# Sigmoid attention with a bilinear feed-forward network: every engine's work in a written order, decoding of the weights dealt out in single operations, no GpSimd work, the first group of products over 28 bursts

## The chip, the cores and the metric

One core of a Trainium2 chip runs the whole program. The metric is the time of one execution on the device in microseconds (us), the median of several runs. "Span" is the time from the first to the last instruction in the one profiled execution.

## What is computed

Attention over 8 batches, 12 heads, 448 positions and 64 values a head, with a sigmoid in the softmax's place; then a network of four weight matrices without a nonlinearity but the product of two branches.

```python
scores = q @ k.transpose(0, 1, 3, 2) / np.sqrt(64) - np.log(448)
attn   = 1.0 / (1.0 + np.exp(-scores))
x      = (attn @ v).transpose(0, 2, 1, 3).reshape(8 * 448, 768)
out    = ((x @ w1) * (x @ w2)) @ w3 @ w_out       # w1, w2: 768x1024, w3: 1024x1024, w_out: 1024x768
```

The four weights arrive as 64-bit numbers, which the kernel reads as pairs of 32-bit words and decodes itself.

## The kernel before

**Attention.** The work is cut into 168 items: for each batch and each quad of four heads seven items of one 128-row chunk for two heads, one of them (`None`) the short last chunk of all four heads. A burst is two items; 84 bursts run, numbered from 0. In each burst TensorE (PE) makes the scores of its items (`scores` L161, `short_scores` L171), ScalarE (ACT) makes two sigmoids (`sigmoid` L151), and PE multiplies the sigmoids of the burst before with v (`attend` L184, `attend_short` L192). A matrix goes to PE as a rounded high part and the rest as a low part (`split`, L66 and L67); `split_pair` does it for q and k on VectorE (DVE).

**The operands of the first products.** When a pair of heads is done, `combine` copies it out of PSUM on ACT (L215) and makes with DVE the sums and differences of blocks (L218) that seven products in Strassen's manner want (`PRODUCTS`: A11, S2, A12, S3, S1, A22, S4). Each is split into high and low (`split_operand`); for `kc == 1` the low part is made by GpSimd (POOL). For the groups after the first, all but the last wait in the list `due`, and six a burst are taken from it in bursts without products.

**The first products.** Two batches are a group, four groups in all. `up` makes for each of 8 column chunks seven products of nine matmuls (L342), so 504 a group. After each product DVE or ACT reads the sum out of PSUM (L324, L327, L350, L356); two PSUM banks, or four with the last group, take turns, so the reading of a product has to be over when the second product after it starts. Results go to memory (`g_dram`, L328). Groups begin at bursts 23, 44 and 65 and run over 16 bursts with 32 matmuls a burst; the fourth follows the last burst.

**The weights.** `prepare_weights` loads raw words of w1 and w2 (L71), ACT takes the magnitude (`magnitude`, L76), DVE decodes in six operations (`decode`, L83 to L99), DVE makes four differences (L268), and seven split operands (ACT's cast, POOL's low part) are stored to `w_dram` (L285 loads them again for each group through a ring of 7 buffers). One step of this stream is a whole decoding or a whole split. `load_job` and `decode_job` do the like for w3 and w_out in 32 jobs from burst 37 on: a load in one burst, and in the next the magnitude, the decoding and the store (L302).

**Order.** PE and the transfer queue of SyncE (SP) run in the order in which the code is written (`manual_schedule(engines={ET.PE, ET.SP})`); DVE, ACT and POOL are ordered by the scheduler. On SP an instruction that waits holds up all transfers written behind it.

**After the groups.** The weights of w3 and w_out are multiplied with each other (L602), and seven products in Strassen's manner give the output (L727).

## Time and profile before

| | |
|---|---|
| runs | 1127.82, 1128.65 and 1133.06 us, median 1128.65 |
| profiled execution, its own time | 1130.64 us |
| its span | 1128.5 us |
| its mean granted TensorE clock | 0.961 of full speed |
| bytes moved | 226.40 MB, mean 201 GB/s |

The profile has for each engine the time in which it was busy, and for each wait what ended it. Matmuls overlap, so PE's busy time is not a measure of how near it is to its peak: a stretch is judged by how far apart equal pieces of its work start. A wait costs only where PE comes to stand still behind it.

### The profile page before, as it was taken

How to read it: one execution, taken by the hardware profiler on the slowest of the kernel's cores; microseconds unless marked ns; L12 is line 12 of the kernel's file. 1: busy time of each engine (PE TensorE's matmuls, PEld its weight loads, DVE VectorE, ACT ScalarE, POOL GpSimd, SP SyncE). 2: the span in 40 equal slices, each digit the busy share in tenths (PEclk: the TensorE clock that was granted, in tenths of full speed). 3: DMA queues.
4: the chain of work that ended last, by engine and by line, in shares of the span. 5: the costliest groups of instructions: out<-in, count | busy, mean ns of one | idle time of the engine just before them, and what ended most of it. 6: DMA issues, size and time to landing. Idle time of an engine off the chain costs nothing.

```text
span 1128.5 us, 14274 instructions
## 1 busy us (share of the span) xinstructions
PE 1016.1 (90%) x5250; PEld 769.3 (68%) x5250; DVE 677.6 (60%) x1038; ACT 367.1 (33%) x518; POOL 125.1 (11%) x88
## 2 busy tenths in 40 slices
PE   7786897679977899898879999989999999999998
PEld 4232565557744666665456676669999999999997
DVE  6898676753586544457854545774444665656663
ACT  4575333333242232323423223321112342323230
POOL 0446223340120000001200000110000000000000
PEclk9899998989998899999889999989999999999999
DMA  6964987978734877766377777638874203344312
GB/s 201 305 218 153 316 275 252 323 265 297 223 106 126 289 255 238 240 190 210 98 258 250 240 245 245 197 121 294 293 255 156 103 9 115 131 139 149 121 49 74
DMA packets 122437, 226.40 MB, mean 201 GB/s; under 512 B 10752, under 2 KB 80384, under 8 KB 122368
## 3 DMA queue, kind: packets, MB, share of 16 engines
q1 hardware_dynamic: 122368, 225.49, 60.0%
q8 instruction: 42, 0.69, 0.3%
q14 instruction: 27, 0.22, 0.1%
HBM read 170.39 MB, written 55.05 MB: 200 GB/s over the span
## 4 chain that ended last, share of the span: by engine, by line
PE 59%; DVE 18%; DMA 14%; issue 4%; ACT 2%; SPq 2%; POOL 0%; ACTq 0%; DVEq 0%; POOLq 0%
PE up L342 26%; PE up L727 18%; PE up L602 6%; DMA raw<-w3T 4%; PE av L184 4%; PE sp L161 4%; DMA raw<-w_out 3%; DMA raw<-w 3%; DMA w<-w_dram 2%; DVE raw L96 2%; DVE f L91 2%; DVE raw L83 2%; DVE f L99 2%; ACT f L76 1%; DVE f L88 1%
## 5 line engine op out<-in xcount | busy, mean ns | idle before, releaser
L342 PE MATMUL up<-hS,w 128*128 128x448 f32 x768 | 248.1, 382 | 52.0 <-DVE u L324 18.2
L151 ACT ACTIVATE a<-sp,bias 128x896 f32<-128x896 f32 x168 | 162.4, 1005 | 228.2 <-PE sp L161 204.7
L342 PE MATMUL up<-hA,w 128*128 128x448 f32 x576 | 188.2, 380 | 21.9 <-ACT p L350 10.4
L342 PEld LDWEIGHTS up<-hS,w 128*128 128x128 f32 x768 | 148.3, 194 | 87.0 <-DVE u L324 22.4
L727 PE MATMUL up<-gh,wo 128*128 128x448 f32 x672 | 192.2, 367 | 0.0
L342 PE MATMUL up<-lS,w 128*128 128x448 f32 x384 | 145.2, 378 | 1.2 <-POOL lS L67 0.8
L342 PEld LDWEIGHTS up<-hA,w 128*128 128x128 f32 x576 | 110.9, 193 | 46.8 <-ACT p L350 11.9
L727 PEld LDWEIGHTS up<-gh,wo 128*128 128x128 f32 x672 | 126.1, 188 | 11.3
L184 PE MATMUL av<-a,vv 128*64 128x448 f32 x576 | 132.2, 574 | 0.0
L727 PE MATMUL up<-gl,wo 128*128 128x448 f32 x336 | 123.2, 367 | 0.0
L342 PE MATMUL up<-lA,w 128*128 128x448 f32 x288 | 108.8, 378 | 0.0
L324 DVE TENSOR_TENSOR u<-up,p 128x448 f32<-128x448 f32 x64 | 39.8, 622 | 104.1 <-PE up L342 103.3
L83 DVE TENSOR_SCALAR raw<-raw 128x768 uint32<-128x768 uint32 (+2 forms) x48 | 25.8, 538 | 100.1 <-ACT f L76 100.0
L161 PE MATMUL sp<-high 64*128 64x448 f32 x288 | 65.5, 450 | 20.0 <-ACT a L151 16.9
L342 PEld LDWEIGHTS up<-lS,w 128*128 128x128 f32 x384 | 74.7, 195 | 12.1 <-issue 4.2
L184 PEld LDWEIGHTS av<-a,vv 128*64 128x64 f32 x576 | 35.0, 141 | 68.5 <-issue 68.5
L161 PEld LDWEIGHTS sp<-high 64*128 64x128 f32 x288 | 28.5, 194 | 68.9 <-ACT a L151 40.2
L76 ACT ACTIVATE f<-raw 128x768 f32<-128x768 f32 (+2 forms) x48 | 34.0, 708 | 122.4 <-DMA raw<-w_out 31.2
L67 POOL TENSOR_TENSOR lA<-A,hA 128x448 fp32r<-128x448 f32 x12 | 21.2, 1764 | 457.3 <-DVE hA L66 457.3
L727 PEld LDWEIGHTS up<-gl,wo 128*128 128x128 f32 x336 | 63.1, 188 | 5.6
L342 PEld LDWEIGHTS up<-lA,w 128*128 128x128 f32 x288 | 55.8, 194 | 10.9 <-issue 6.3
L67 DVE TENSOR_TENSOR gl<-gf,gh 128x896 fp32r<-128x896 f32 x40 | 41.9, 1087 | 31.3 <-ACT gh L66 31.3
(78 smaller groups left out, 1348.2 us busy)
## 6 DMA issues: line engine op xcount, KB each, us to landing
w<-w_dram SPq DMA_DIRECT2D x224, 384.0 KB, 4.7
w_dram<-wo SPq DMA_DIRECT2D x56, 384.0 KB, 4.4
g_dram<-c SPq DMA_DIRECT2D x64, 224.0 KB, 2.6
gf<-g_dram SPq DMA_DIRECT2D x16, 896.0 KB, 5.4
raw<-w SPq DMA_DIRECT2D x16, 768.0 KB, 8.6
qk<-qT SPq DMA_DIRECT2D x48, 224.0 KB, 4.5
qk<-kT SPq DMA_DIRECT2D x48, 224.0 KB, 4.7
out<-o_sb SPq DMA_DIRECT2D x48, 224.0 KB, 2.0
```

The lines of the kernel that those rows point to most:

```text
L67: lo_engine.tensor_tensor(out=dst_lo, in0=src, in1=dst_hi, op=ALU.subtract)
L76: nc.scalar.activation(f, raw[..., 1].bitcast(F32), AF.Abs, scale=HW_SCALE)
L83: nc.vector.tensor_scalar(out=high, in0=high, scalar1=0x80000000, scalar2=0x80000000, op0=ALU.bitwise_and, op1=ALU.bitwise_xor,)
L91: nc.vector.scalar_tensor_tensor(out=fb, in0=fb, scalar=3, in1=high, op0=ALU.logical_shift_left, op1=ALU.bitwise_xor)
L96: nc.vector.scalar_tensor_tensor(out=r, in0=low, scalar=2.0 ** -52, in1=r, op0=ALU.mult, op1=ALU.mult)
L151: nc.scalar.activation(dst, src, AF.Sigmoid, bias=bias[:n], scale=scale)
L161: nc.tensor.matmul(sp[:, j], k[rows, 1, at:at + P], q[rows, 0], start=m == 0, stop=m == 2)
L184: nc.tensor.matmul(acc[cols, :S], vv[:, c, at:at + D], a[:, j], start=u == 0 and c == 0, stop=u == 1 and c == NC - 2,)
L324: nc.vector.tensor_tensor(out=out, in0=a, in1=b, op=ALU.add)
L342: nc.tensor.matmul(a, w[:, i, kc], x, start=bool(start) and kc == 0 and m == 0, stop=bool(stop) and kc == KH - 1 and m == 2, skip_group_ch ...
L602: nc.tensor.matmul(acc, a[:, jc], w[:, jc, ms], start=(jc == 0 and m == 0), stop=(jc == NF - 1 and m == 2),)
L727: nc.tensor.matmul(acc, w[:, fc, ms], g[:, fc], start=start and fc == 0 and m == 0, stop=fc == NH - 1 and m == 2, skip_group_check=True,)
```

## The change

All five engines keep the written order until the last group is out. POOL gets no work; its low parts go to DVE. `decode` gives up control after each of its six operations, and so do the differences and splits of the weights (`finish_weights`). Outside the products two such single operations are taken a burst; beside the first group `beside` takes 3 or 4 behind each product's sum, and beside the second and third group two operations of w3's and w_out's decoding (`prepare_rest`) or one operand of the list `groups`. The casts of the first group's operands and every second one of the others' move to ACT, and so does q's and k's high part in bursts with products. The groups run over bursts 25 to 52, 58 to 66 and 71 to 79, with 18, 56 and 56 matmuls a burst. The weights' ring has 6 buffers instead of 7, `c11` and `c22` one instead of two, and the stores of results are issued one product later.

```diff
-        split(high, low, qk, nc.vector.tensor_copy, nc.vector)
+        split(high, low, qk, hi_engine, nc.vector)
...
     def split_operand(g, name, kc, src):
-        split(h, l, src, nc.vector.tensor_copy, nc.gpsimd if kc == 1 else nc.vector)
+        turn = g > 0 and len(ops[g]) % 2
+        split(h, l, src, nc.vector.tensor_copy if turn else nc.scalar.copy, nc.vector)
...
+    def late(g, kc):
+        a11, a12, s1, a22 = (xf.pop((g, name, kc)) for name in ("A11", "A12", "A21", "A22"))
+        split_operand(g, "S1", kc, s1)
+        yield
+        total(a11, s1, a11, ALU.subtract)
+        split_operand(g, "S2", kc, a11)
+        yield
+        if g > 0:
+            split_operand(g, "A12", kc, a12)
+            yield
+        total(a12, a12, a11, ALU.subtract)
+        split_operand(g, "S4", kc, a12)
+        yield
+        split_operand(g, "A22", kc, a22)
+        yield
...
     def prepare_weights():
...
+                for step, _ in enumerate(decode(raw[i], f)):
+                    if step == 4 and (i, fc) != (1, NF - 1):
+                        nxt = magnitude(raw[1 - i], p1, 3)
+                    if step == 5 and fc + 1 < NF:
+                        raw[i] = load(fc + 1, i)
+                    yield
+                    for _ in range(2 if (i, step) != (0, 0) else 1):
+                        if next(extras, None):
+                            yield
+            take(extras, 100)
+            extras = finish_weights(fc, fs)
...
-                split(wo[:, 0], wo[:, 1], src, nc.scalar.copy, nc.gpsimd)
+            split(wo[:, 0], wo[:, 1], src, nc.scalar.copy, nc.vector)
...
-    RING = 7
+    RING = 6
...
+        for i, (_, dst) in enumerate(jobs):
+            for step, _ in enumerate(decode(raw[i % 2], f)):
+                if step == 0 and store:
+                    nc.sync.dma_start(out=store[0], in_=store[1])
+                if step == 2 and i + 1 < len(jobs):
+                    following = magnitude(raw[(i + 1) % 2], p2[0], 3)
+                yield
+            store = dst, f
+            raw[i % 2] = load(i + 2)
+            f = following
...
-    order.enter_context(tc.manual_schedule(engines={ET.PE, ET.SP}))
+    ALL = {ET.PE, ET.SP, ET.Activation, ET.DVE, ET.Pool}
+    order.enter_context(tc.manual_schedule(engines=ALL))
...
+    spans = ((25, 53), (58, 67), (71, 80))
+    CHANGE = 53
...
+    def beside(g, n):
+        if not take(change, 1):
+            if g == 0:
+                take(weights, 3 + n % 5 % 2)
+            else:
+                take(rest, 2)
...
+        for g, (at, end) in enumerate(spans):
+            if k == at:
+                filler = up(g)
+            if at <= k < end:
+                n = GROUP * (k + 1 - at) // (end - at) - GROUP * (k - at) // (end - at)
+                take(filler, n + (10 if k == end - 1 else 0))
+                if k == end - 1:
+                    change = groups(g + 1)
+                break
+        else:
+            take(change, 4)
+            take(weights, 2)
```

What moves is best seen in the instructions of an engine as they stand in its queue. DVE in the second group of products, before (`u` and `c` are the sums of the products, `raw` and `f` the decoding):

```order
L324 TENSOR_TENSOR u_3455<-up,p 128x448
L83 TENSOR_SCALAR raw<-raw 128x512
L88 TENSOR_SCALAR f<-f 128x512
L91 SCALAR_TENSOR_TENSOR f<-f,raw 128x512
L95 TENSOR_SCALAR raw<-f 128x512
L96 SCALAR_TENSOR_TENSOR raw<-raw 128x512
L99 TENSOR_TENSOR f<-f,raw 128x512
L83 TENSOR_SCALAR raw<-raw 128x384
L324 TENSOR_TENSOR u_3529<-up,p 128x448
```

and now:

```order
L398 TENSOR_TENSOR u_3605<-up,p 128x448
L93 SCALAR_TENSOR_TENSOR f<-f,raw 128x512
L98 TENSOR_SCALAR raw<-f 128x512
L100 SCALAR_TENSOR_TENSOR raw<-raw 128x512
L104 TENSOR_TENSOR f<-f,raw 128x512
L398 TENSOR_TENSOR u_3637<-up,p 128x448
L83 TENSOR_SCALAR raw<-raw 128x512
L89 TENSOR_SCALAR f<-f 128x512
L67 TENSOR_TENSOR low<-qk,high 128x896
L398 TENSOR_TENSOR c_3680<-up,u_3637 128x448
L93 SCALAR_TENSOR_TENSOR f<-f,raw 128x512
L98 TENSOR_SCALAR raw<-f 128x512
```

Before, seven operations of decoding stand between two sums; now two behind each product, so four where ACT reads the sum between (`low` is a part of q and k).

SP's queue in the second group, before (L285 loads the operands of products, L71 raw words, L302 stores decoded ones, L126 is q and k):

```order
L302 DMA w_dram<-f 128x512
L71 DMA raw<-w3T 128x4x256
L126 DMA qk<-qT 128x448
L126 DMA qk<-kT 128x448
L126 DMA qk<-qT 128x448
L126 DMA qk<-kT 128x448
L285 DMA w<-w_dram 128x768 x4
L302 DMA w_dram<-f 128x512
L285 DMA w<-w_dram 128x768 x2
```

and now (L344, L71 and L367 in the same parts; L411 stores results):

```order
L71 DMA raw<-w3T 128x4x256
L367 DMA wo_dram<-f 128x384
L344 DMA w<-w_dram 128x768 x2
L139 DMA vv<-vL 128x3x256
L145 DMA vs<-vL 64x128 x2
L344 DMA w<-w_dram 128x768
L71 DMA raw<-w3T 128x4x256
L367 DMA wo_dram<-f 128x384
L344 DMA w<-w_dram 128x768 x3
L411 DMA g_dram<-c_4137 128x448
```

The store of a decoded job stood ahead of the next raw load and, here, of four loads of operands, and waited for the last operation of its own decoding; it now comes one job later, behind the raw load, which waits for that operation instead of it.

ACT at the end of the second batch, in the first stage, before (`A` is an operand's copy, `a` a sigmoid, `wo` the high part of a weight):

```order
L151 ACTIVATE a<-sp,bias 128x896 x2
L215 COPY A_855<-av 128x448
L151 ACTIVATE a<-sp,bias 128x896 x2
L66 CAST wo<-t_794 128x384
L66 CAST wo<-f 128x384
L151 ACTIVATE a<-sp,bias 128x896 x2
L215 COPY A_940<-av 128x448
L66 CAST wo<-t_796 128x384
```

and now (`hS` and `hA` are the high parts of operands):

```order
L156 ACTIVATE a<-sp,bias 128x896 x4
L246 COPY A_876<-av 128x448
L66 CAST hS_879<-A_648 128x448
L66 CAST hS_884<-A_283 128x448
L66 CAST hS_889<-A_463 128x448
L66 CAST hA_893<-A_876 128x448
L156 ACTIVATE a<-sp,bias 128x896 x2
L246 COPY A_927<-av 128x448
```

The four casts of a finished pair of heads stand now between the copy and the sigmoids of the next burst; before they were DVE's.

## Rows read from the trace of the kernel before

**Rows 1.** The busy time by engine, from the page: us, share of the span, number of instructions.
```profile
PE 1016.1 (90%) x5250; PEld 769.3 (68%) x5250; DVE 677.6 (60%) x1038; ACT 367.1 (33%) x518; POOL 125.1 (11%) x88
```

**Rows 2.** Busy time in the eight stages of the program: start and end in us, length, busy us and number of instructions of PE, PEld, DVE, ACT and POOL, then the granted clock as a share of full speed, the share of the DMA engines and GB/s.
```profile
6.30:115.50 109.20, 85.18 (x497) 34.75 (x496) 94.32 (x125) 65.00 (x88) 48.49 (x28) 0.91 0.68 223
115.50:315.90 200.40, 169.93 (x856) 122.74 (x854) 122.40 (x175) 66.61 (x100) 47.82 (x39) 0.93 0.80 272
315.90:336.50 20.60, 16.59 (x111) 6.90 (x110) 16.84 (x32) 10.99 (x15) 5.54 (x4) 1.00 0.44 134
336.50:525.60 189.10, 165.11 (x852) 118.90 (x852) 102.08 (x186) 51.97 (x71) 5.19 (x4) 0.95 0.68 221
525.60:548.20 22.60, 19.05 (x111) 7.97 (x110) 18.81 (x33) 12.17 (x15) 6.38 (x4) 0.85 0.38 116
548.20:728.30 180.10, 163.04 (x854) 117.77 (x852) 103.19 (x190) 51.09 (x71) 6.06 (x4) 0.97 0.70 230
728.30:748.00 19.70, 16.17 (x92) 7.64 (x91) 17.06 (x30) 7.64 (x10) 5.38 (x4) 0.95 0.24 74
748.00:1128.50 380.50, 376.25 (x1880) 349.09 (x1880) 200.63 (x268) 100.17 (x147) 0.00 (x0) 0.99 0.43 148
```

**Rows 3.** PE's timeline, the first scores of five bursts: start, us, engine, line, instruction, how many. The first two are the start of a burst with products and that of the next; the other three are the starts of two bursts without products and of the next, where the second begins with the scores of a short chunk (L171).
```profile
646.85 0.47 PE L161 MATMUL sp<-high 64*128 64x448 f32 x2
656.61 0.47 PE L161 MATMUL sp<-high 64*128 64x448 f32 x2
...
728.31 0.48 PE L161 MATMUL sp<-high 64*128 64x448 f32 x2
731.39 0.98 PE L171 MATMUL sp<-qk 64*64 64x448 f32 x8
734.76 0.47 PE L161 MATMUL sp<-high 64*128 64x448 f32 x2
```

**Rows 4.** The timeline around one stall in the second group of products, for SP's queue, ACT, DVE and PE; in brackets stand the idle time before a row and what ended it.
```profile
362.93 0.34 SPq L302 DMA_DIRECT2D w_dram<-f  x1
363.37 0.38 SPq L71 DMA_DIRECT2D raw<-w3T  x1
365.82 2.20 SPq L285 DMA_DIRECT2D w<-w_dram  x4
...
367.71 0.66 ACT L76 ACTIVATE f<-raw 128x512 f32<-128x512 f32 x1 [10.20 <-DMA raw<-w3T]
...
363.46 0.63 DVE L327 TENSOR_TENSOR c<-u,c 128x448 f32<-128x448 f32 x1
368.40 0.43 DVE L83 TENSOR_SCALAR raw<-raw 128x512 uint32<-128x512 uint32 x1 [4.31 <-ACT f L76]
...
371.14 0.71 PE L342 MATMUL up<-hS,w 128*128 128x448 f32 x1 [8.41 <-DVE raw L96]
```

**Rows 5.** The waits of ACT for raw words: who for whom, us in total, times, longest us.
```profile
ACT f L76 <- DMA raw<-w_out: 31.2, 10, 5.9
ACT f L76 <- DMA raw<-w3T: 29.3, 10, 10.2
ACT f L76 <- DMA raw<-w: 27.8, 12, 8.2
```

**Rows 6.** The timeline of POOL and of DVE in the first stage (start, us).
```profile
61.39 1.80 POOL L67 TENSOR_TENSOR wo<-t,wo 128x384 fp32r<-128x384 f32 x1 [1.97 <-issue]
...
62.26 1.36 DVE L83 TENSOR_SCALAR raw<-raw 128x768 uint32<-128x768 uint32 x1
63.54 0.55 DVE L95 TENSOR_SCALAR raw<-f 128x768 uint32<-128x768 uint32 x1
64.00 0.55 DVE L88 TENSOR_SCALAR f<-f 128x768 f32<-128x768 f32 x1
64.47 0.95 DVE L96 SCALAR_TENSOR_TENSOR raw<-raw 128x768 f32<-128x768 uint32 x1
```

**Rows 7.** The timeline of DVE between the first and the second group of products, starts one behind another.
```profile
328.29 1.08 DVE L67 TENSOR_TENSOR low<-qk,high 128x896 fp32r<-128x896 f32 x1
329.29 0.68 DVE L99 TENSOR_TENSOR f<-f,raw 128x512 f32<-128x512 f32 x1
329.89 0.62 DVE L218 TENSOR_TENSOR A<-A,A 128x448 f32<-128x448 f32 x1
330.43 0.39 DVE L66 CAST hA<-A 128x448 fp32r<-128x448 f32 x1
330.73 0.62 DVE L218 TENSOR_TENSOR S<-A,A 128x448 f32<-128x448 f32 x1
```

**Rows 8.** Two groups of ACT by line and shape: busy us, mean ns of one | idle time before, and what ended it.
```profile
L151 ACT ACTIVATE a<-sp,bias 128x896 f32<-128x896 f32 x168 | 162.4, 1005 | 228.2 <-PE sp L161 204.7 <-PE sp L171 23.0
...
L215 ACT COPY A<-av 128x448 f32<-128x448 f32 x48 | 25.5, 531 | 10.0 <-PE av L192 6.9 <-PE av L184 2.9
```

**Rows 9.** Transfers: what, how many, KB each, median us from issue to landing.
```profile
w<-w_dram SPq DMA_DIRECT2D x224, 384.0 KB, 4.7
...
raw<-w SPq DMA_DIRECT2D x16, 768.0 KB, 8.6
```

**Rows 10.** The two stretches of 40 us with the most traffic under products (columns as in rows 2).
```profile
240.00:280.00 40.00, 39.35 (x204) 28.82 (x205) 13.58 (x19) 13.38 (x20) 6.35 (x6) 0.95 0.90 323
760.00:800.00 40.00, 40.00 (x195) 36.34 (x194) 17.43 (x27) 7.21 (x11) 0.00 (x0) 1.00 0.87 296
```

More of the change, by code (lines that the diff above doesn't have):

```diff
@@ L249, in sigmoid_attention_bilinear_ffn, with load @@
     PRODUCTS = ("A11", "S2", "A12", "S3", "S1", "A22", "S4")
-    def load_first(fc):
-        return [load_words(words(w, slice(fc * P, (fc + 1) * P)), p1) for w in (w1, w2)]
     def prepare_weights():
-        raw = load_first(0)
+        def load(fc, i):
+            return load_words(words((w1, w2)[i], slice(fc * P, (fc + 1) * P)), p1)
+        extras = iter(())
+        raw = [load(0, i) for i in range(2)]
+        yield
+        nxt = magnitude(raw[0], p1, 3)
         for fc in range(NF):
@@ new lines, in prepare_weights, with finish_weights, subtract, store @@
+            take(extras, 100)
+            extras = finish_weights(fc, fs)
+        while next(extras, None):
+            yield
+    def finish_weights(fc, fs):
+        b11, b21, b12, b22 = (f[:, h * KH:(h + 1) * KH] for f in fs for h in range(2))
+        made = []
+        def subtract(name, in0, in1, out=None):
+            if out is None:
+                out = p1.tile([P, KH, P], F32, name=name, bufs=1)
+            total(out, in0, in1, ALU.subtract)
+            return out
+        def store():
+            k, wo = made.pop(0)
+            nc.sync.dma_start(out=w_dram[fc * 7 + k], in_=wo.bitcast(F32))
+            stored.add(fc * 7 + k)
+        def divide(k, src):
+            if len(made) > 1:
+                store()
+            wo = p1.tile([P, 2, KH, P], F32R, name="wo", bufs=3)
+            split(wo[:, 0], wo[:, 1], src, nc.scalar.copy, nc.vector)
+            made.append((k, wo))
+        divide(0, b11)
+        yield 1
+        t3 = subtract("t3", b22, b12)
+        yield 1
+        t1 = subtract("t1", b12, b11, b12)
+        yield 1
+        divide(2, b21)
+        yield 1
+        t2 = subtract("t2", b22, t1)
+        yield 1
+        n4 = subtract("n4", b21, t2)
+        yield 1
+        for k, src in ((1, t2), (3, t3), (4, t1), (5, n4), (6, b22)):
+            divide(k, src)
+            yield 1
+        store()
+        yield 1
+        store()
@@ L283, in load_weights @@
         if n < NG * NF * 7:
+            while n % (NF * 7) not in stored:
+                next(weights)
             ring[n] = pm.tile([P, 2, KH, P], F32R, name="w", bufs=RING)
@@ L327, in leave @@
                 nc.vector.tensor_tensor(out=out, in0=a, in1=out, op=ALU.mult)
[L328 removed]
+                stores.append((g_dram[fc, :, at[b]], out))
             for k, name in enumerate(PRODUCTS):
@@ L333, in up @@
                 w = ring.pop(n)
+                while any((name, kc) not in ops[g] for kc in range(KH)):
+                    next(change)
+                for dst, src in stores:
+                    nc.sync.dma_start(out=dst, in_=src)
+                stores.clear()
                 bank, start, stop = ((0, 1, 0), (1, 1, 0), (0, 0, 1), (1, 0, 1),
@@ L368, in up @@
                     leave(2 * g, u2, c11)
+                beside(g, n)
                 yield
+        for dst, src in stores:
+            nc.sync.dma_start(out=dst, in_=src)
     def take(stream, n):
-        for _ in range(n):
-            next(stream, None)
+        done = 0
+        for _ in itertools.islice(stream, n):
+            done += 1
+        return done
     ET = mybir.EngineType
     order = ExitStack()
-    order.enter_context(tc.manual_schedule(engines={ET.PE, ET.SP}))
+    ALL = {ET.PE, ET.SP, ET.Activation, ET.DVE, ET.Pool}
+    order.enter_context(tc.manual_schedule(engines=ALL))
     zeros = p1.tile([P, 512], F32R, name="wo", bufs=3)
@@ L418, in sigmoid_attention_bilinear_ffn @@
     filler = iter(())
+    change = rest = iter(())
     accs = {}
@@ L462, in sigmoid_attention_bilinear_ffn @@
             p2.append(phase_2.enter_context(tc.tile_pool(name="p2", bufs=2, side="right")))
+            rest = prepare_rest()
+        beside_up = any(at <= k < end for at, end in spans)
+        hi_cast = nc.scalar.copy if beside_up else nc.vector.tensor_copy
         burst = items[2 * k:2 * k + 2]
         for t, x in burst:
-            prepare(t, x)
+            prepare(t, x, hi_cast)
         now = []
```

152 lines of the change are left out of this document (64 added, 88 removed).

## The prediction

> **What bounds the kernel now.** I read the page's busy times first, then the stages, then the starts of bursts. PE is busy for 90% of the span, DVE for 60%, ACT for 33%, POOL for 11% [rows 1]; whether PE is also the bound has to be seen by stage [rows 2]. The last stage, the fourth group and everything behind it, is PE at full clock, 376.25 of 380.5 us. The seven stages ahead of it take 748 us, and there PE loses time. A burst of attention alone takes 731.39 - 728.31 = 3.08 us, or 3.37 with a short chunk, and 60 and 24 of the 84 are of each kind: 3.16 on average [rows 3]. A burst with 32 matmuls of products takes 9.76 us undisturbed [rows 3], so one matmul costs (9.76 - 3.08) / 32 = 0.209 us, and a group of 504 costs 105 us. By these prices 84 bursts and three groups are 265 + 316 = 581 us. With the 6.3 us before the first burst that makes 587, against 748: PE waits for 161 us, in every stage some.
>
> What it waits for shows in one stall [rows 4]. SP's queue held the store of a decoded job until 362.93, when DVE had finished its decoding. Only then went out the raw load of the next job, 363.37, and four loads of operands, from 365.82. ACT had waited 10.2 us for the raw words when they came, DVE 4.31 us for ACT, and PE 8.41 us until 371.14. (The trace names a DVE operation as the releaser; that operation was over for half a microsecond, and the loads just issued are the likelier one.) In all, ACT waited 31.2 + 29.3 + 27.8 = 88 us in 32 waits for raw words, 2.8 us each [rows 5].
>
> **The change, stage by stage.** I split the new order into the stages it makes.
>
> *POOL's work to DVE, all stages.* 56 low parts of weights and 32 of operands come to DVE. DVE's operations of 768 columns start 0.46 to 0.47 us apart when alone, and the same kind took 1.36 us while POOL worked, from 61.39 to 63.19 [rows 6]. Operations of 448 columns start 0.54 us apart, casts 0.30, q's and k's low part 1.00 [rows 7]. So DVE gets 56 x 0.47 + 32 x 0.54 = 44 us, and its operations are no longer stretched. By starts, with half of the decoding's operations at the 0.95 us of the dearer kind, its new load is 74 us in the first stage and 115 us beside the first group's decoding (42 sums, 66 of decoding, 42 low parts, 24 differences, 17 for q, k and totals): it fits under PE in both, so I cost it at nothing there. If DVE is stretched again by something, that cover is thin in the first stage only.
>
> *First stage, bursts 0 to 24.* PE's floor is 25 x 3.16 = 79 us. At each of three finished pairs of the second batch ACT's next sigmoids now stand behind four casts that take turns with DVE: a copy and four casts on ACT at 0.53 each [rows 8], three totals and two low parts of 0.62 between [rows 7], and eight crossings at some 0.03 to 0.05 (ACT ended at 368.37, DVE began at 368.40 [rows 4]) are 6.1 us; with a sigmoid of 1.0 [rows 8] a burst becomes 7.2 us, 4.1 over its floor: 12 us. What else is lost lies between nothing and the 36 us of before (109.2 less 23 x 3.16). I take 13: the landing of the first raw words, 8.6 us [rows 9], which ACT awaits in both orders ahead of the second burst's sigmoids, and some 4 for the crossings, nearer to the low end since DVE had 94 us of work here [rows 2] and now 74. The stage ends at 6.3 + 79 + 12 + 13 = 110 us.
>
> *First group, bursts 25 to 52.* A burst has 18 matmuls, 3.16 + 18 x 0.209 = 6.92 us, and 28 are 194. While the weights are still prepared, for 43 products in 21.5 bursts (149 us), SP moves 43 loads and 48 stores of 384 KB, 10 raw loads of 768 KB [rows 9] and 11 MB of q, k, v and results: 54.9 MB, so 369 GB/s would be needed. The two busiest stretches under products had 323 and 296 GB/s [rows 10], in which PE hardly waited. So here the transfers are the bound. Bounds: 323 gives 170 us, the 272 GB/s that this work had in all of the first group's stage [rows 2] gives 202. I take the mean of the two busiest, 310: 177 us. The other 6.5 bursts are 45: together 222, the stage ends at 332.
>
> The Trainium skill, "SBUF — State Buffer", section "A bandwidth-pool intuition that's wrong", gives some 358 GB/s between HBM and one core. By it the 54.9 MB would take 153 us and the whole would be 24 us less than I forecast. No stretch of this trace reaches it.
>
> *Between the groups, bursts 53 to 57, 67 to 70, 80 to 84.* Four operands a burst: by starts DVE has 21 low parts, 10 casts, 9 totals and the parts of q and k, 24.7 us, then 20.9 and 20.1. PE's floors are 15.8, 12.6 and, with the chain up to the fourth group, about 17. DVE binds: 25 + 20 + 22 (two for the last chain, which runs across ACT and DVE as in the first stage). Before these stretches took 20.6 + 22.6 + 19.7 [rows 2].
>
> *Second and third group, 9 bursts each.* 56 x 0.209 + 3.16 = 14.87 us a burst, 134 a group. DVE has 56 sums at 0.54 and 106 operations of decoding at 0.60 or less [rows 7], with some 6 for the rest 100 us at most, under it; and a pair of decoding operations, up to 1.2 us, fits behind each sum within the 1.9 us until the next product ends. The raw load is out as soon as its buffer is read, the decoding that needs it comes three products later, 5.6 us of PE, and its landing took 5 to 9 [rows 4, 9]; so ACT's magnitude may wait, at times with a copy of a sum behind it. In the second group 43.9 MB must move, at 310 GB/s 142 us; with 5 for the first raw load, which nothing precedes, 147. In the third it is 39.6 MB, 128 us, under PE; 14 jobs at 0.4 (a copy 1.3 us late in two of seven products) make it 140. For such a job the bounds are 0 and the 2 us that one cost before: the third group's stage was 180.1 against 16 x 3.16 + 105 = 156 [rows 2], 24 us for some 12 jobs.
>
> *Smaller things, at nothing.* Six ring buffers still load five products ahead, 9 us, for a landing of 4.7 [rows 9]. With one `c11` a result's store has three products' time, 5.6 us, before it is overwritten. If SP is late by several microseconds, both turn into waits of PE.
>
> *Sum.* 110 + 222 + 25 + 147 + 20 + 140 + 22 = 686, for 748 before, so 62 us less. The profiled execution took 1130.64 us, 2 above the median of the runs, so I take the difference from the median: 1128.65 - 62 = 1067 us. A measurement of this kernel can tell some 0.5%, 5.6 us, from no change.
>
> **The rivals.**
> *Transfers are slower than in the best stretches.* At 272 GB/s the first group's decoding takes 202, the second group 161, the third 146: 25 + 14 + 6 = 45 more, 1112 us. For it: stores and loads go through one queue that waits in order. Against it: 323 was reached with PE 98% busy.
> *PE alone binds.* No loss in the first stage but the chains (-13), 170 us for the decoding (-7), 136 and 134 in the groups (-17), 6 less between: 43 less, 1024 us. For it: before, undisturbed bursts at the floor came in long rows.
> *A fixed order passes every late raw load on.* A magnitude that waits for its words now holds ACT, behind it the copies and casts, behind those DVE's sums, behind those PE; before, the scheduler put them where it saw room. 42 raw loads come beside or after the first group's start. At the 2.8 us that ACT waited each time [rows 5] they cost 116, of which my sum has 11: 1172 us. The point at which it decides is (62 + 11) / 42 = 1.7 us a load: above it, slower than before. For it: the stall of 8.41 us was of this kind [rows 4]. Against it: loads go out earlier, and two operations instead of seven stand between sums.
> The Trainium skill, "TensorE: Matmul & The Clock Gate", section "Architectural detail: the array is 16× 32×32, not 1× 128×128", says that ACT and DVE take their instructions strictly first in, first out; by that rule this rival has its full price, and the trace agrees in that DVE stood still for 4.31 us behind one operation [rows 4].
> *The dealing does not do what it says.* If what was lost beside products comes back between them (the three stretches grow to some 40 us each, the first stage to 120), 60 us return: about 1127, no change.
>
> **How the numbers follow.** My forecast 0.45, slower transfers 0.20, PE alone 0.15, late loads passed on 0.15, no effect 0.05. Faster by over 0.5%: 0.45 + 0.20 + 0.15 less 0.01 for the tail of the slow transfers, 0.79; within: 0.05; slower: 0.16. The range goes from the case of PE alone, 1028, over that of slow transfers to 1130, with 15 for its own spread; left out are late loads and half of no effect.
>
> **What would show it.** Right: the second and third group start at about 357 and 524 us, their bursts are 15 to 16.5 us apart, the fourth group starts at about 686; DMA near 300 GB/s and 85% from 110 to 290 us; no POOL time, DVE's operations of 768 columns at 0.55 or 0.95 us throughout; bursts of 7 us three times before 110. Wrong: ACT's waits for raw words followed by PE's waits for sums, several microseconds each, in the second and third group; or a first group over 250 us with DMA under 80%.

## The result and the profile after

The changed kernel takes 1086.33 us (median of four runs, 1083.99 to 1087.23), the kernel before 1130.51 beside it: ratio 0.9606, 95% interval 0.9575 to 0.9638. That is faster, inside the range of 1028 to 1130, and 19 us above the forecast of 1067. The profiled execution has a span of 1083.8 us, 44.7 less than before, where 62 were forecast; the missing 17 are looked for in the stages.

The busy time by engine, from the page of the kernel after, answers to [rows 1]:

```profile
PE 1004.1 (93%) x5250; PEld 766.4 (71%) x5250; DVE 650.3 (60%) x1042; ACT 410.7 (38%) x598; POOL 0.2 (0%) x4
```

DVE took over 84 operations of POOL (56 low parts of weights and 28 of operands; the four that POOL keeps take 0.2 us) and gave 80 casts to ACT. It is busy for 27 us less, also since its operations are no longer stretched as in [rows 6]. The stages of the kernel after, columns as in [rows 2]:

```profile
6.10:114.30 108.20, 90.92 (x542) 39.09 (x541) 71.49 (x108) 72.95 (x100) 0.00 (x0) 0.89 0.60 198
114.30:349.10 234.80, 208.36 (x1116) 137.27 (x1114) 133.95 (x213) 110.73 (x161) 0.00 (x0) 0.93 0.77 266
349.10:371.60 22.50, 17.86 (x109) 7.23 (x108) 19.93 (x35) 13.61 (x21) 0.00 (x0) 0.92 0.44 134
371.60:511.70 140.10, 135.92 (x700) 106.94 (x700) 94.75 (x181) 44.20 (x66) 0.00 (x0) 0.99 0.85 289
511.70:529.30 17.60, 13.16 (x89) 5.76 (x88) 16.48 (x31) 11.12 (x17) 0.00 (x0) 0.94 0.61 190
529.30:672.80 143.50, 138.50 (x704) 108.22 (x704) 88.63 (x165) 42.33 (x64) 0.00 (x0) 0.97 0.78 257
672.80:698.00 25.20, 18.60 (x111) 8.71 (x110) 20.65 (x39) 14.64 (x23) 0.00 (x0) 0.93 0.14 46
698.00:1083.80 385.80, 376.17 (x1881) 349.80 (x1881) 202.12 (x270) 99.67 (x147) 0.00 (x0) 0.99 0.43 147
```

| stage | forecast | measured |
|---|---|---|
| bursts 0 to 24, with the 6 us ahead | 110 | 114.3 |
| first group, 25 to 52 | 222 | 234.8 |
| 53 to 57 | 25 | 22.5 |
| second group, 58 to 66 | 147 | 140.1 |
| 67 to 70 | 20 | 17.6 |
| third group, 71 to 79 | 140 | 143.5 |
| up to the fourth group's unbroken run | 22 | 25.2 |
| the rest | 380.5 | 385.8 |

The largest miss is the first group, and its row contradicts the reason given for it: PE stood still for 26 of the 235 us, yet the transfers ran at 266 GB/s, less than before, and not at 310. PE's timeline shows how it was lost, the first scores of five bursts in a row (columns as in [rows 3], in brackets the wait and what ended it):

```profile
138.73 0.47 PE L166 MATMUL sp<-high 64*128 64x448 f32 x2
145.64 0.47 PE L166 MATMUL sp<-high 64*128 64x448 f32 x2
160.26 0.74 PE L166 MATMUL sp<-high 64*128 64x448 f32 x2 [7.08 <-ACT a L156]
169.69 0.47 PE L166 MATMUL sp<-high 64*128 64x448 f32 x2
176.61 0.47 PE L166 MATMUL sp<-high 64*128 64x448 f32 x2
```

Three bursts keep the forecast's 6.92 us to within 0.02 (138.73 to 145.64, 169.69 to 176.61 and the next). One takes 14.62, the one behind it 9.43. Such a pair, or one like it, comes once in every three to four bursts up to burst 40, about once for each column chunk of the weights. ACT, DVE and SP in the same stretch of the kernel after:

```profile
150.09 0.51 ACT L66 CAST wo<-f 128x384 fp32r<-128x384 f32 x1 [0.41 <-DMA w_dram<-wo]
...
151.07 0.51 ACT L66 CAST wo<-n 128x384 fp32r<-128x384 f32 x1
158.79 0.51 ACT L66 CAST wo<-f 128x384 fp32r<-128x384 f32 x1 [7.21 <-DMA w_dram<-wo]
159.21 1.90 ACT L156 ACTIVATE a<-sp,bias 128x896 f32<-128x896 f32 x2
...
151.11 0.95 DVE L104 TENSOR_TENSOR f<-f,raw 128x768 f32<-128x768 f32 x1
...
159.33 0.56 DVE L67 TENSOR_TENSOR wo<-f,wo 128x384 fp32r<-128x384 f32 x1 [6.80 <-ACT wo L66]
...
152.09 0.38 SPq L71 DMA_DIRECT2D raw<-w  x1
152.57 0.97 SPq L306 DMA_DIRECT2D w_dram<-wo  x2
```

Read from the bottom. SP's raw load waits for DVE's last decoding operation (L104, done at 152.06); behind it, at 152.57, go out two stores of split weights. One of them empties the buffer `wo` that the chunk's last split wants. There are three such buffers, and a store is issued two splits behind its own split, so one split ahead of the buffer's next use; splits stand 1 us apart here (150.09, 151.07), a store lands after 5.1 us (the median; 4.4 before). ACT's cast therefore stands still for 7.21 us, behind it the sigmoids (159.21), behind those PE, and on DVE a low part (159.33) with a product's sum behind it. The burst after the stall ran with a granted clock of 0.73, partly at the lower of the two levels (1.2 and 2.4 GHz), after PE had stood for 7.08 us; the one after that had 1.00 again. Over the whole kernel after, the waits that belong together (columns as in [rows 5]):

```profile
ACT wo L66 <- DMA w_dram<-wo: 64.7, 22, 7.4
PE sp L166 <- ACT a L156: 37.8, 12, 7.1
ACT f L76 <- DMA raw<-w3T: 43.9, 11, 8.1
ACT f L76 <- DMA raw<-w_out: 37.7, 11, 8.4
```

### The profile page after: what moved, and what is told of

It is laid out like the page before. It is cut to its first block, busy times and chain, and to the rows that moved or that the text cites. A ratio compares the mean times of both kernels' runs of the same rounds, so it can differ in the third digit from the quotient of the medians.

```text
span 1083.8 us, 14159 instructions
## 1 busy us (share of the span) xinstructions
PE 1004.1 (93%) x5250; PEld 766.4 (71%) x5250; DVE 650.3 (60%) x1042; ACT 410.7 (38%) x598; POOL 0.2 (0%) x4
## 4 chain that ended last, share of the span: by engine, by line
PE 50%; DVE 5%; DMA 1%; ACT 1%; issue 1%; SPq 0%; DVEq 0%; ACTq 0%
PE up L421 21%; PE up L827 19%; PE up L702 6%; PE av L189 1%; PE sp L166 1%; DMA w<-w_dram 1%; DVE lS L67 1%; DVE A L214 1%; DVE lA L67 1%; DVE u L398 0%; PE sp L176 0%; DVE hS L66 0%; PE av L197 0%; ACT a L156 0%; DVE low L67 0%
## 5 line engine op out<-in xcount | busy, mean ns | idle before, releaser
L421 PE MATMUL up<-hS,w 128*128 128x448 f32 x768 | 244.2, 377 | 30.0 <-DVE u L398 13.1
L421 PEld LDWEIGHTS up<-hS,w 128*128 128x128 f32 x768 | 146.7, 192 | 64.1 <-DVE u L398 14.6
L421 PE MATMUL up<-hA,w 128*128 128x448 f32 x576 | 183.6, 372 | 3.4 <-ACT p L429 3.2
L421 PEld LDWEIGHTS up<-hA,w 128*128 128x128 f32 x576 | 109.5, 190 | 25.5 <-issue 7.8
L166 PE MATMUL sp<-high 64*128 64x448 f32 x288 | 65.9, 454 | 37.9 <-ACT a L156 37.8
L398 DVE TENSOR_TENSOR u<-up,u 128x448 f32<-128x448 f32 x64 | 39.8, 622 | 42.4 <-PE up L421 41.7
L67 DVE TENSOR_TENSOR low<-qk,high 128x896 fp32r<-128x896 f32 x48 | 52.3, 1090 | 20.2 <-ACT high L66 16.1
```

Source lines behind the costliest of these rows:

```text
L67: lo_engine.tensor_tensor(out=dst_lo, in0=src, in1=dst_hi, op=ALU.subtract)
L166: nc.tensor.matmul(sp[:, j], k[rows, 1, at:at + P], q[rows, 0], start=m == 0, stop=m == 2)
L398: nc.vector.tensor_tensor(out=out, in0=a, in1=b, op=ALU.add)
L421: nc.tensor.matmul(a, w[:, i, kc], x, start=bool(start) and kc == 0 and m == 0, stop=bool(stop) and kc == KH - 1 and m == 2, skip_group_ch ...
```

## The experiments

Each ratio is to the kernel before, measured on the same chip, where that kernel's median was 1130.5 to 1134.7 us; medians in us, "changed" is the kernel after, "2" the kernel of experiment 2.

| edit | on | median | ratio (95%) |
|---|---|---|---|
| (changed kernel itself) | | 1086.3 | 0.9606 (0.9575 to 0.9638) |
| 1 four `wo` | changed | 1050.2 | 0.9268 (0.9215 to 0.9322) |
| 2 store one split later | changed | 1050.9 | 0.9273 (0.9225 to 0.9320) |
| 3 casts to DVE | changed | 1081.6 | 0.9541 (0.9483 to 0.9600) |
| 4 w3 early | changed | 1084.0 | 0.9575 (0.9521 to 0.9629) |
| 5 no POOL | before | 1117.0 | 0.9848 (0.9821 to 0.9875) |
| 6 store a job later | before | 1116.8 | 0.9844 (0.9790 to 0.9898) |
| 7 DVE, ACT by scheduler | changed | 1026.3 | 0.9051 (0.9021 to 0.9080) |
| 8 differences first | 2 | 1040.6 | 0.9169 (0.9135 to 0.9204) |
| 9 edits 2, 7 and 8 | changed | 1028.7 | 0.9083 (0.9039 to 0.9128) |
| 10 six operations in a heap | 2 | 1100.0 | 0.9717 (0.9659 to 0.9775) |
| 11 first group over 16 bursts | 2 | 1073.2 | 0.9482 (0.9442 to 0.9523) |
| 12 POOL's low parts back | 2 | 1048.5 | 0.9258 (0.9223 to 0.9293) |

**1 and 2. Is it the store or the bandwidth?**

```diff
-            wo = p1.tile([P, 2, KH, P], F32R, name="wo", bufs=3)
+            wo = p1.tile([P, 2, KH, P], F32R, name="wo", bufs=4)
...
-    RING = 6
+    RING = 5
...
```

> Edit: four buffers wo instead of three for the split weights, and, to make room for the fourth, a ring of five weight buffers w instead of six. Theory 1 (the first group is late because a split's cast on ACT waits for the landing of the store of the buffer's last use, 64.7 us in 22 waits, and holds ACT's sigmoids and with them PE): a buffer is now free one split earlier, some 2 to 7 us; the stalls of 7 us at each column chunk go, the first group's stage falls from 234.8 us to 200 to 210, and the whole to about 1055 (1045 to 1065); ACT's wait for DMA w_dram<-wo falls under 20 us. Theory 2 (the transfers' bandwidth binds there, as I forecast): the same 54.9 MB have to move, the stage stays within 6 us, the whole at 1080 or more, and the time goes to PE's waits for w instead. The smaller ring alone, by landings of 4.7 us for 4 products of 1.8 us ahead, should cost nothing where transfers are undisturbed.

```diff
-            if len(made) > 1:
+            if made:
                 store()
...
         store()
         yield 1
-        store()
```

> Edit: the store of a split weight is issued one split later instead of two, buffers unchanged. Theory 1 (landing of stores holds ACT's casts): each store is issued one step of the weights' stream earlier, about 1.9 us or more, and is out of the buffer by so much sooner; of the some 8 stalls of 7 us in the first group most shrink: stage 234.8 us to 205 to 220, the whole 1057 to 1072. But SP may now stand at a store whose low part isn't finished, with loads queued behind it; that would show as PE's waits for w. Theory 2 (bandwidth binds): within 6 us of 1086.

Two different edits of the same wait each take some 36 us away, as theory 1 says. The first group of experiment 1 up to burst 52, then until about its last store of weights, then 40 us of it, and last the kernel after until about its own last store (columns as in [rows 2]):

```profile
107.60:308.40 200.80, 198.25 (x1116) 131.73 (x1114) 133.04 (x213) 110.96 (x161) 0.00 (x0) 1.00 0.88 311
...
107.60:265.00 157.40, 154.85 (x870) 102.98 (x869) 122.38 (x198) 93.14 (x139) 0.00 (x0) 1.00 0.93 335
...
120.00:160.00 40.00, 40.00 (x230) 26.63 (x228) 30.27 (x51) 22.25 (x33) 0.00 (x0) 1.00 0.97 354
```
```profile
114.30:304.00 189.70, 164.49 (x868) 108.15 (x867) 121.61 (x196) 89.83 (x134) 0.00 (x0) 0.92 0.80 277
```

157.4 us at 335 GB/s and 189.7 at 277 are both some 52.6 MB: the same bytes, 32 us sooner, with PE 98% busy meanwhile. So the bandwidth did not bind the changed kernel. The stage comes to 200.8 us, 7 over PE's floor of 194. Of the 34 us that it loses against the kernel after, 24 are time in which PE stood still; the other 10 are matmuls that take longer (208.4 against 198.3 us busy, at a mean granted clock of 0.93 against 1.00). Another 7 us go in the first stage, most of them where the same wait stood once (bursts 15 and 16). ACT's wait for these stores falls from 64.7 to 21.2 us. The 40 us at 354 GB/s with PE busy throughout lie near the some 358 between HBM and one core that the Trainium skill, "SBUF — State Buffer", section "A bandwidth-pool intuition that's wrong", gives. As a limit the trace does not bear it out: the same run has 366 GB/s from 201 to 241 us and 390 from 196 to 216, and the kernel before, for which the prediction says that no stretch reaches the figure, has 402 from 241 to 251. (The view counts a few per cent too much in short stretches: its share of the DMA engines is 1.01 to 1.05 there.)

**7 and 9. The written order of DVE and ACT.**

```diff
-    order.enter_context(tc.manual_schedule(engines=ALL))
+    order.enter_context(tc.manual_schedule(engines={ET.PE, ET.SP}))
```

> Edit of the changed kernel: only PE and SP keep the written order, as before the change; DVE and ACT are ordered by the scheduler again; all else (dealing, stores, no GpSimd, 28 bursts) stays. Theory 1 (the given order is what keeps two decoding operations, not seven, between two sums): the scheduler heaps operations up again, second and third group grow from 140.1 and 143.5 us by 10 us or more each, the whole 1100 to 1120. Theory 2 (the code's order already sets the scheduler's priorities; the store late and the dealing do it): within 6 us of 1086. A third way: the scheduler moves sigmoids ahead of casts that wait for a store, and the first group, 234.8 us, falls by 20 us or more, the whole below 1070.

The third way came out, with a gain that I had not put so high: 60 us below the changed kernel. Only experiment 9, which has the same edit in it, is as fast. ACT still waits for the stores of `wo`; what changed is what stands behind the wait. ACT and PE in experiment 7:

```profile
136.72 0.51 ACT L66 CAST wo<-t 128x384 fp32r<-128x384 f32 x1 [5.80 <-DMA w_dram<-wo]
...
134.12 0.47 PE L166 MATMUL sp<-high 64*128 64x448 f32 x2
```

ACT stands for 5.80 us, its sigmoids had been made before, and PE goes on through it: a burst's scores (134.12) begin in the middle of it without a wait. The waits of experiment 7 over the whole kernel:

```profile
ACT wo L66 <- DMA w_dram<-wo: 56.9, 32, 5.8
...
PE sp L166 <- ACT a L156: 11.5, 11, 2.5
```

ACT waits for these stores nearly as long as in the kernel after (64.7), PE for sigmoids 11.5 us instead of 37.8. The stages, from the first group to the start of the fourth's run:

```profile
104.80:312.90 208.10, 199.40 (x1114) 131.37 (x1112) 144.37 (x239) 116.38 (x171) 0.00 (x0) 1.00 0.88 307
312.90:329.00 16.10, 16.10 (x109) 6.87 (x108) 9.05 (x15) 11.47 (x15) 0.00 (x0) 1.00 0.51 159
329.00:468.80 139.80, 135.69 (x702) 105.80 (x700) 93.59 (x185) 47.56 (x72) 0.00 (x0) 1.00 0.89 295
468.80:482.10 13.30, 13.13 (x89) 5.66 (x88) 13.30 (x25) 9.40 (x12) 0.00 (x0) 1.00 0.53 175
482.10:620.90 138.80, 135.06 (x704) 105.84 (x702) 87.52 (x167) 42.33 (x63) 0.00 (x0) 1.00 0.82 271
620.90:640.70 19.80, 17.94 (x110) 8.88 (x109) 14.45 (x28) 12.73 (x18) 0.00 (x0) 1.00 0.18 60
```

Against the changed kernel: 9 us in the first stage, 27 in the first group, 16 in the three stretches between and around (16.1, 13.3 and 19.8 for 22.5, 17.6 and 25.2, the first two close to PE's floors of 15.8 and 12.6), 5 in the second and third group, 5 at the end: 62, the difference of the spans. The second and third group, for which I thought the order was needed, did not lose without it. Experiment 9 asks whether the gains add:

> Edit: the changed kernel with three edits of earlier experiments together: DVE and ACT ordered by the scheduler, the store of a split one split later, the differences ahead of the splits. Theory 1 (the order's 60 us and the store's 35 us are the same stall met from two sides: with the sigmoids free to pass, a late store no longer holds PE): the gains don't add, 1018 to 1028. Theory 2 (they are different losses): under 1005, which is near the sum of PE's floors, 581 + 6 + 380 + 24 = 991. Theory 3 (with the buffers free sooner the scheduler heaps work before the sums): over 1028.

The gains do not add, as theory 1 says: 0.9083 against 0.9051. The median of 1028.7 lies 0.7 above theory 1's range, where theory 3 begins (four runs, 1024.6 to 1031.7), but the second and third group, 139.2 and 140.6 us, show no heaps. PE waits for sigmoids 13.1 us there. With the sigmoids free to pass, a late store costs PE next to nothing, and taking it away brings nothing.

**3 and 8. The chain ahead of the first group.**

```diff
-        turn = g > 0 and len(ops[g]) % 2
+        turn = len(ops[g]) % 2 if g > 0 else name in ("S1", "S2", "S4", "A22")
```

> Edit: the 12 casts of the first group's operands S1, S2, S4 and A22 of the three pairs finished last go back from ACT to DVE, in bursts 17 to 24. Theory 1 (the excess of 18.3 us in bursts 19 to 23 is the chain of copy, four casts on ACT with three differences on DVE between, ahead of the next sigmoids): ACT's sigmoids come at once behind the copy, the excess goes by 8 to 15 us, the first group starts at 100 to 106 instead of 114.3, the whole 1072 to 1078. Theory 2 (DVE's queue is as near to the bound there, and its operations are merely in another place): within 3 us of 1086.

Neither theory: the first group starts at 111.8 instead of 114.3, and the whole is some 5 us faster, with intervals that overlap a little. ACT's sigmoids no longer wait, but the high part of q and k (on DVE from 105.80 to 106.42) comes late, which PE wants as well; PE in experiment 3:

```profile
106.56 0.74 PE L166 MATMUL sp<-high 64*128 64x448 f32 x2 [4.44 <-DVE high L66]
```

The chain moved to the other queue. So experiment 8 shortens it instead:

```diff
-        split_operand(g, "S1", kc, s1)
-        yield
         total(a11, s1, a11, ALU.subtract)
+        if g == 0:
+            total(a12, a12, a11, ALU.subtract)
+        split_operand(g, "S1", kc, s1)
+        yield
         split_operand(g, "S2", kc, a11)
...
             split_operand(g, "A12", kc, a12)
             yield
-        total(a12, a12, a11, ALU.subtract)
+            total(a12, a12, a11, ALU.subtract)
```

> Edit of the kernel of the experiment with the store one split later (1050.9 us): the differences that S2 and S4 are made of come ahead of the splits, so ACT's four casts stand behind one another instead of taking turns with DVE's difference and low part (three turns of 1.80 us each). Theory 1 (this chain of 7.2 us ahead of the sigmoids makes the excess of 18 us in bursts 19 to 23): the chain falls to about 3 us, the excess by 6 to 12 us, the whole to 1039 to 1045. Theory 2 (q's and k's parts behind the chain on DVE bind just as well, as they did when the casts were DVE's): at most 3 us, 1048 or more.

As theory 1 says: 0.9169 against 0.9273, 10 us between the medians, and the first group starts at 100.4 instead of 108.0. ACT's chain in the kernel after, then in experiment 8:

```profile
97.06 0.53 ACT L246 COPY A<-av 128x448 f32<-128x448 f32 x1
99.65 0.57 ACT L66 CAST hS<-A 128x448 fp32r<-128x448 f32 x1 [2.07 <-DVE A L214]
101.44 0.56 ACT L66 CAST hS<-A 128x448 fp32r<-128x448 f32 x1 [1.23 <-DVE A L214]
103.24 0.56 ACT L66 CAST hS<-A 128x448 fp32r<-128x448 f32 x1 [1.23 <-DVE A L214]
103.71 0.56 ACT L66 CAST hA<-A 128x448 fp32r<-128x448 f32 x1
```
```profile
85.89 0.53 ACT L248 COPY A<-av 128x448 f32<-128x448 f32 x1
88.83 1.88 ACT L66 CAST hS<-A 128x448 fp32r<-128x448 f32 x3 [2.42 <-DVE A L214]
90.62 0.56 ACT L66 CAST hA<-A 128x448 fp32r<-128x448 f32 x1
```

After, two further casts come 1.80 us apart, as DVE makes a low part (0.54) before the next difference (0.62) that the cast (0.57) waits for; in experiment 8 three casts run in 1.88 us. From the copy to the last cast's end it is 7.2 us and 5.3, where 3 were expected; the rest is q's and k's part on DVE ahead of the first total, which stayed.

**10. The dealing.**

```diff
-                take(rest, 2)
+                take(rest, 6 if n % 3 == 0 else 0)
```

> Edit of the kernel of the experiment with the store one split later (1050.9 us), in given order: beside the second and third group the decoding comes as six operations behind every third product instead of two behind each. Theory 1 (heaps of decoding between two sums are what PE waits for; six take 3.4 us, a sum may be 1.9 us late at most): some 1.5 us at each of 32 jobs, the two stages, 137.6 and 145.1 us, grow by 20 us or more each, the whole 1085 to 1105. Theory 2 (the second and third group are bound by late raw words and transfers, whose work is the same): within 6 us of 1051.

The time is theory 1's: 1100, 49 us slower (the profiled execution, the slowest of four, has a span of 1105.0, 59 more). The second and third group of experiment 10, against 137.6 and 145.1 us in experiment 2:

```profile
335.90:507.70 171.80, 146.83 (x701) 112.19 (x701) 95.97 (x182) 44.00 (x67) 0.00 (x0) 0.93 0.71 236
...
530.70:692.90 162.20, 143.38 (x704) 109.63 (x704) 87.77 (x162) 41.54 (x63) 0.00 (x0) 0.96 0.70 227
```

With the stretch between them (23.0 us for 17.5) 57 us are gone, 1.8 for each of 32 jobs, with DVE's busy time as in experiment 2: 38 us in which PE waits longer, and 19 by which its matmuls take longer at a lower granted clock. The number comes close to what the kernel before lost here, 57 us (189.1 + 180.1 - 312), but the way is another. PE's waits in experiment 10 from 336 to 693 us (columns as in [rows 5]), and one of them with ACT's wait behind it:

```profile
PE up L420 <- ACT p L428: 14.2, 5, 4.5
PE up L420 <- ACT c L434: 12.2, 7, 3.4
PE up L420 <- DVE u L397: 12.1, 10, 2.9
```
```profile
386.08 0.66 ACT L76 ACTIVATE f<-raw 128x512 f32<-128x512 f32 x1 [8.55 <-DMA raw<-w3T]
...
387.22 0.74 PE L420 MATMUL up<-hA,w 128*128 128x448 f32 x1 [4.53 <-ACT p L428]
```

Theory 1 meant the sums on DVE behind a heap; PE waits for these 15.6 us (12.1 and 3.5). For sums that ACT copies it waits 26.4 us, where experiment 2 has 6.8. In the heap no product lies between a raw load (issued at 381.67) and the magnitude that reads it (386.08): ACT's waits for raw words of w3 and w_out grow from 72 to 152 us, and the copies of sums stand behind them. So the heaps cost this much with ACT in a fixed order, and more of PE's longer waits stand behind ACT than behind DVE. In the kernel before, ACT's order was the scheduler's; there PE waited 22.6 us for DVE's sums in the two groups and 4.0 for ACT's.

**5 and 6. Two parts of the change alone, on the kernel before.**

```diff
-        split(h, l, src, nc.vector.tensor_copy, nc.gpsimd if kc == 1 else nc.vector)
+        split(h, l, src, nc.vector.tensor_copy, nc.vector)
...
-                split(wo[:, 0], wo[:, 1], src, nc.scalar.copy, nc.gpsimd)
+                split(wo[:, 0], wo[:, 1], src, nc.scalar.copy, nc.vector)
```

> Edit of the kernel before, one part of the change alone: the low parts that GpSimd made go to DVE; nothing else, DVE, ACT and POOL still ordered by the scheduler. Theory 1 (DVE's operations of 768 columns take up to 1.36 us beside POOL instead of 0.55, and POOL's own 1.4 to 1.8 us stand in the path of the weights' buffers): the first stage, 109.2 us, loses 8 to 15 us, the first group's 200.4 us some 5, the whole 1110 to 1120. Theory 2 (DVE is not what binds before; 44 us more work in its queue take back what the unstretched operations give): 1125 to 1135.

Theory 1 holds for the first stage, which takes 98.4 us instead of 109.2, and for the whole, 17.6 us less. The first group keeps its 200.7 (200.4).

```diff
+        store_job()
...
-        nc.sync.dma_start(out=jobs[i][1], in_=decode(raw, magnitude(raw, p2[0])))
+        done.append((jobs[i][1], decode(raw, magnitude(raw, p2[0]))))
```

(`store_job` issues the oldest entry of `done`.)

> Edit of the kernel before, one part of the change alone: the store of a decoded w3 or w_out job is issued one job later, so that the raw load and the loads of products' operands written behind it don't wait on SP for the decoding. Theory 1 (the stall of 8.41 us was this wait, and its kind makes most of what the second and third group lose, 33 and 24 us): the two stages, 189.1 and 180.1 us, come to 170 to 178 and 166 to 172, the whole to 1095 to 1110. Theory 2 (the losses come from the decoding itself, seven operations in one piece between two sums): within 5 us of before, 1125 to 1135.

The result lies between the theories, and its four runs lie 11 us apart (1111.1 to 1122.5). The second and third group of experiment 6, in the fastest of them:

```profile
331.70:514.00 182.30, 165.81 (x854) 119.25 (x852) 99.76 (x182) 51.66 (x71) 21.11 (x7) 0.96 0.69 223
534.90:711.20 176.30, 161.69 (x854) 116.47 (x852) 99.56 (x184) 50.62 (x70) 20.11 (x7) 0.99 0.70 223
```

They gain 7 and 4 us of the 57, and some 5 lie ahead of them. The stall of [rows 4] was real, but its kind was the smaller share of the loss. What is left fits decoding in heaps: PE still waits 18.3 us for DVE's sums there.

**11 and 12. Two parts undone on experiment 2.**

```diff
-    spans = ((25, 53), (58, 67), (71, 80))
+    spans = ((25, 41), (58, 67), (71, 80))
```

> Edit of the kernel of the experiment with the store one split later: the first group over 16 bursts, 25 to 40, with 32 matmuls a burst as before the change, instead of 28 with 18. Theory 1 (the decoding's transfers and DVE's operations have 2.8 us a product instead of 3.5, less than DVE's 2.7 plus its waits and than 350 GB/s allow): bursts 25 to 40 take 180 to 195 us against a floor of 156, bursts 41 to 57 their 55 to 60, the whole 1070 to 1090. Theory 2 (the spread costs PE nothing and gives it nothing, since no engine is full): within 6 us of 1051.

This is theory 1 in the main numbers: bursts 25 to 40 take 189.5 us for a floor of 156, bursts 25 to 57 253.8 instead of 225.7, the whole 22 us more. (Bursts 41 to 57 take 64.3, not 55 to 60.) That stretch ran at 302 GB/s, so transfers alone didn't set it; which of DVE, ACT and the stores did was not separated.

```diff
-            split(wo[:, 0], wo[:, 1], src, nc.scalar.copy, nc.vector)
+            split(wo[:, 0], wo[:, 1], src, nc.scalar.copy, nc.gpsimd)
```

> Edit of the kernel of the experiment with the store one split later: the low parts of the 56 split weights are made by GpSimd again instead of DVE, in given order. Theory 1 (an operation there takes 1.4 to 1.8 us and stretches DVE's to 1.36 us while it runs, and the store behind it is later): first stage and first group, 108.0 and 202.5 us, grow by 10 to 30 us together, the whole 1060 to 1080. Theory 2 (DVE is relieved of 26 us, which pays for the stretch): within 6 us of 1051.

As theory 2 says, there is no difference (0.9258 and 0.9273). An operation on POOL takes some 1.15 us here. Relieving GpSimd was worth 17.6 us in the kernel before (weights and operands), and for the weights' part it is worth nothing in the new order.

**4. The end.**

```diff
+    load_w3(0)
+    load_w3(1)
     for jc in range(NF):
...
-    load_w3(0)
-    load_w3(1)
```

> Edit: the two loads of w3 for the last part are issued ahead of the loop that prepares them, where a load of w_out stood, instead of directly before the split that reads them. Theory 1 (the stall at 779 to 790 us, after the last attention burst, is DVE's low part of w3 waiting for ACT's high part, which waits for a load issued at 779.4 and landed 5.8 us later, with the products' sums behind it): the stall of some 10 us goes, the whole is about 1077, and the products of w3 and w_out start some 9 us earlier. Theory 2 (PE would then wait for the fourth group's operands or sums anyway): within 3 us of 1086.

There is no difference, as theory 2 says. The stall is gone, as theory 1 says, but another came. PE's longest wait inside the fourth group in the kernel after, then in experiment 4:

```profile
790.16 0.74 PE L421 MATMUL up<-hS,w 128*128 128x448 f32 x1 [5.32 <-DVE c L398]
```
```profile
714.45 0.44 PE L421 MATMUL up<-hS,w 128*128 128x448 f32 x1 [3.30 <-DMA w<-w_dram]
```

The two loads of w3 now go out ahead of six loads of the products' operands, and PE waits for those. In the ten us around it (709.5 to 719.5) the granted clock was 0.83, as in the ten us around the kernel after's wait (785 to 795). From the matmul with which the run starts to the first product of w3 and w_out 109.4 us pass in the kernel after (from 697.99) and 109.5 here.

## Why the prediction was right, and where it was not

*What carried the gain was named rightly, its mechanism in part.* The second and third group lose 16 us over PE's floors (283.6 - 268; 19 were forecast), where they lost 57 before: 41 of the 44.7 us. Experiment 10 shows that this hangs on the dealing: heaped up again, the operations take 49 to 57 us back. It does not show that DVE's heap between two sums is the way, as the prediction has it, since more of PE's longer waits there stood behind ACT, which waited for raw words; that the same 57 come out is partly luck. Experiment 7 shows that the written order of ACT and DVE is not what it hangs on. That each of these groups now runs over 9 bursts instead of 16 was not undone by itself.

Of the signs that it named, POOL does nothing, and DVE's operations of 768 columns keep 0.55 and 0.95 us. The bursts of both groups stand 14.6 to 17.9 us apart (15 to 16.5 forecast) but for one of 21. Three signs did not come: DMA "near 300 GB/s and 85%" from 110 to 290 us (273 and 0.78), the starts at 357, 524 and 686 (371.6, 529.3 and 698.0), and three bursts of 7 us before 110 (8.0, 5.6 and 9.3).

*The step that failed* is in the first group: "So here the transfers are the bound", with 177 us at 310 GB/s for 54.9 MB. The bytes were nearly right (some 52.6 MB in the stretches above), the bound was not. The rate came from [rows 10], whose stretches are not the two with the most traffic: the kernel before has 334 GB/s from 236 to 276 us and 322 from 186 to 226. Without the stalls these bytes pass in 157 us at 335 GB/s and the stage is 201 us, PE's 194 and a little; the stalls bring it to 235. The forecast of 222 lies between, too high for transfers and with nothing for the stalls. The list of smaller things priced the rings of `w` and `c11`, not the three `wo`, though the trace of before had the landing, 4.4 us, and the new order the distance: single splits behind one another.

*The first stage's chain was mis-sized*: 12 us forecast for three pairs, 18.3 measured as excess over the floors of bursts 19 to 23. The three bursts that the chain lengthens (8.02, 5.55 and 9.33 us) are 13.4 over their floors, near the forecast, though unlike each other. The other 4.9 are in bursts 20 and 23, each behind a wait of PE (4.16 and 4.13 us): they take 5.59 and 5.60 us at a granted clock of 0.54, so almost wholly at the lower level, and the forecast had nothing for them. From the copy to the last cast the chain takes 7.2 us where 6.1 were reckoned; experiment 8 shows that the turns with DVE's low parts are part of it, and q's and k's parts ahead in DVE's queue the rest.

*The rivals.* "A fixed order passes every late raw load on" fell as it was put: ACT waited 3.7 us each for 22 raw loads of w3 and w_out, yet the second and third group lost only 283.6 - 268 = 16 us, 0.5 for each of 32 jobs; the point of decision was 1.7. Experiment 10 shows that its mechanism is real: where no product lies between the load and the magnitude, PE waits for ACT's copies. And it was right for another transfer, the store of `wo`, in another stage. Experiment 7 shows this: nearly the same waits of ACT, with sigmoids free to pass, leave PE 26 us less of waiting for them. By the Trainium skill's rule of strict order on ACT and DVE ("TensorE: Matmul & The Clock Gate", the section the prediction names) that is what had to follow, and here the trace agrees (the sigmoids behind the cast that stood for 7.21 us); the rule says nothing of who writes the order. "PE alone binds", 1024 us, came true where the written order of ACT and DVE was taken back: 1026. So one part of the change gives back more than half of what the others gain.

*The three stretches between* were taken as bound by DVE, and were near it in the changed kernel. Experiment 7 has less DVE work in them (9.05 us for 19.93 in the first), since its scheduler had done part of it earlier, and reaches PE's floor.

*The end* was forecast unchanged and took 5 us more. Counted from the same matmul to the first product of w3 and w_out, it is 109.4 us, where the kernel before has 105.2 and experiment 7 has 104.8; so the loss comes with the written order of ACT and DVE. Experiment 4 shows that the wait for w3 alone is not the cause; which waits add up there stays open.

*Numbers of the working.* POOL had 28 low parts of operands, not 32, so DVE gets 41 us by the prediction's prices, not 44. The lower end of the range, 1028, is called the case of PE alone, whose own sum is 1024.

## What to carry to other kernels

When an engine's order is fixed, price every ring of buffers by the time between two uses of one buffer in the new order against the landing of the transfer that empties it, not by its count. Put work that others wait for (here sigmoids and sums) ahead of the operation that may wait for memory, or leave that engine to the scheduler and fix only the queues whose order matters. Leave work of other engines between a load and the operation in a fixed order that waits for it. A rate that the transfers showed under stalls is no bound; the same bytes ran a fifth faster once PE no longer stood still.

## What was not expected of the hardware

Under matmuls that left PE no gap for 40 us, the transfers of one core reached 354 GB/s, above the 323 of [rows 10]. The landing of a 384 KB store was 4.4 us in the kernel before, 5.1 after, 5.5 in experiment 2 and 6.1 in experiment 1, where one buffer more covered most of it; the first group's stage moved 272, 266, 308 and 311 GB/s there, so the rate alone does not set it. DVE's operations of 768 columns keep 0.55 and 0.95 us in the changed kernel, as in the stretches of [rows 6] without POOL.
